# Eight single PSUM banks, 128-row FFN tiles for a second block, and a new written-out order in a fused attention and gated FFN kernel

## The chip, the cores and the metric

The kernel runs on one core of a Trainium2 chip, alone. The metric is the device time of one execution in microseconds, the median of three runs. TensorE is called PE in the profile, VectorE DVE, ScalarE ACT, GpSimd POOL and SyncE SP. PEld is the loading of weights into PE.

## The reference

Block-sparse attention (4 batches, 8 heads, 768 tokens, head width 64), and its output, seen as 3072 tokens of 512 channels, goes through a gated feed-forward network with 1536 inner channels. Cut to what matters:

```python
scores = scale * np.matmul(q, k.transpose(0, 1, 3, 2))          # scale = 1/8
# mask of 32 x 32 blocks: band of 1, first and last row and column, 3 random blocks per row
scores = np.where(mask, scores, -1000000000.0)
attn = softmax(scores)                                           # over keys
out = np.matmul(attn, v)
x = out.transpose(0, 2, 1, 3).reshape(3072, 512)
gate = 1.0 / (1.0 + np.exp(-(x @ w_gate)))
val = x @ w_val
return (gate * val) @ w_out
```

Inputs and output are float32; the mask is the same for all batches and heads.

## The kernel before

All arithmetic on PE is in 16-bit floats with 32-bit sums. The work is cut into 12 units: a unit is one batch and 256 of its 768 queries. In a unit the 8 heads go in 4 pairs (`Pair`), and the keys of a pair in 3 steps of 256 (`Step`).

For one step PE computes scores of 256 keys by 256 queries for both heads (`Step.qk`, 4 matmuls of 64 rows; the two heads lie on the two halves of PE's rows and run together). ACT takes the exponential of the 128x1024 result out of PSUM (`exp`, line 586), DVE multiplies it by the 0/1 mask (`mul`, line 592). In unit 0 the mask isn't ready in time, so there PE adds a bias to the scores instead (matmuls `bias,e`) and DVE does not multiply. When three steps of a pair are done, PE multiplies them by the values, which carry a column of ones (`pv` in unit 0 with 128 rows, `pv_parts` from there on with 64 rows and two partial sums, which DVE adds in `fold`, line 646). DVE divides by the ones column (`norm`, lines 655 and 656), and the result is turned into `xT`: by PE and a copy in units 0 and 1, by a transposing DMA on SP's queue from unit 2 on.

The FFN (`Ffn`) takes units in eight groups, four of one unit (256 tokens) and four of two (512 tokens). `f` computes gate and value sums of 128 inner channels at a time (two times 128 for a group of one unit), ACT takes a tanh (line 801), DVE multiplies (`gate`, line 804) into `ht`. `y` multiplies `ht` by `wo` into 256 output rows, ACT or DVE copies the result to `ysb`, and SP stores it. Group 0 uses PE with all 128 rows (`whole`), the others split the 128 rows into halves that write different PSUM banks (`turns`).

PSUM is held as four tiles `m0` to `m3` of two banks each. Everything that PE writes takes a whole tile, however small it is, and gives it back when it has been read: transposes of 64 columns too.

q, k and v of batch 0 and the weights are loaded by POOL's queue in the fixed order of `FIRST`:

```python
FIRST = "k1 q1 k2 q2 k3 q3 v0 v1 v2 v3 r0 w0 r1 w1 r2 w2 r3 w3 w4 w5 o0 o1 o2"
```

`k1` is k of head pair 1, `q1` the first 256 queries of it, `r0` the other 512 queries of pair 0, `w0` 256 channels of `wg` and then of `wv`, `o0` a third of `wo`. Pair 0's k and first queries come in front of these by SP's and ACT's queues. The loads of later batches are tasks like the others; some wait for a score matmul (a gate, `@` in the order).

The program is written as a list of tasks (`plan.add`), numbered as they are added, each with the engines that may do it and a duration used by a planner outside the program. The order in which tasks are issued is the string `ORDER`: `34:1` is task 34 on PSUM tile 1, `4D` task 4 on DVE, `j3` a matmul on zeros that keeps PE busy. An engine does its tasks strictly in this order: a task that waits holds up all that stand behind it on its engine. The numbers in `plan.add` do not enter the program; only `ORDER` and the task functions do.

Of the kernel before, what the change touches and what calls it, by code (L numbers as in the profile page):

```python
# [16 lines left out]
ALU = mybir.AluOpType  # L17
# [14 lines left out]
PE, ACT, DVE, DMA, SP = "PADGS"  # L32
# [4 lines left out]
EARLY = 2  # L37
# [3 lines left out]
j3 j3 j3 j3 j3 j3 j3 j3 5A 8D j3 0 11A j3s 9:0 j3s j3s j3s 10D j3s j3s 12:1 1:2 j3s 13A 3:0 2 j3s 34:1 4D 35 15:2  # L41
j3s 32:3 16D 6:0 33 17:1 7D 117:2 18D 97:0 118D 44:1 98A j3s 22:3 78:2 23D 45 36:0 79D 20:3 37 21D
40:2 25:1 30:3 41 26D 76:0 77D 46:1 31 54:2 19 74:0 47 75D 27:3 24 55 50:0 28D 80:1 64:3 51 81D
48:2 65 60:1 49 56:0 61 14 66:3 58:2 67D 105@30 57 29 89:3 59 38:1 90 52:0 86:2 53D 87 39 68:3
93:0 69D 62:1 108:2 94 42:3 109 43D 102:0 63D 111:3 70:1 103 110 126:2 71D 112 104 95:0 84:1 96D
122:3 85A 113 140:0 127 123 91 130:1 128 132:3 141 129 131 72:2 119:0 99:1 73D 133 120 147:2 134
100 135 142 157:0 148 154:3 171:1 124 155 149 158 88 164:3 143:2 156 176:0 92@164 144 121 146@111
101 172 170@44 165 173 161:2 217@54 145 190:1 177 189@46 162 125@40 178 237@54 159 186:3 191 150:2
115:0 151D 192 174:2 187 116 204:1 175 188 231:0 179:3 183:2 232 205 180D 244:3 184 233 206 166
245 82:0 200:2 218 83D 201 246 234:3 193:0 219 194A 152 235 185 153 211:2 136:0 220 137D 212 138  # L50
272:3 195 139 229 223A 202 167:0 255:2 168 236 273 213 221A 239 214:0 230 307:1 274 169 215 275
256 240 216 197:3 308 257 196 181 198 258 248:0 309 182 199 241:2 249 242 310 268:3 262 225:1 250
260 114@268 263 269 251 252:2 226 318:0 261 207:3 319 253 315:1 208 289:2 316 160@315 254 106:0
265:3 243 290 107A 247@265 266 270 276:1 209 291 300:0 293:3 277 301 278 282:1 294 292 283 297 163
303:0 335:2 295 302 222 304 279 227 285:1 336 296 286 238 359:0 305 337 360 210 284 331:3 228
362:1 348 332 361 264 349 363 333 328:0 287 350 329 267 322:3 351A 320 344:1 353A 311:0 323
203@344 345 341:2 387:3 321@359 312 342 317 271@282 426:1 373:0 313 411@300 427 330 397:2 374 398
343 388 346 375 259 408:1 376 389 355:2 400@268 409 390 347@30 419:0 356 334@89 380:3 405:1 428
370:2 381 306@111 364 420 288@44 406 371 386@214 366:3 421 410 365@265 454:2 422 433:1 455 432@380
# [3 lines left out]
442 474:1 484:0 463A 378 465A 339 467:2 452 340 475 524:3 480 485 525 514 354 515:1 327 468 486  # L63
# [4 lines left out]
538 583 438 550:1 567 571 542 439 586 551 638:0 563:2 572 425 539 564 552 595:1 573A 404 577:2 604  # L68
639 574 596 578 609:0 568 597 555 575A 627:2 598 616:3 610 628 617 543@616 635:1 565 712@200 630:2
611 569@300 636 612 592:3 446@563 688:0 631 593 658@60 689 654 706:1 556@231 588:3 707 579 641@550  # L70
640 642:0 632 676@471 619:1 633 589 587@282 620 594 691@214 623:2 690 613 590 670:1 591 643 671
637 605:3 624 644 621 606 645 659:1 618 625 709:0 681:3 710 626 660 607 655:2 682 692:0 656 453
663:3 711 726@99 661 657 608@234 673:2 693 662 674 622@652 664 672 694 548 699:1 695 665 723:2 666
# [3 lines left out]
762 669 782 730:3 745A 734:0 760 757:2 731 735 753 798:3 703 758 799 732 736 764:0 759 750 743A  # L77
600 765 797 826:3 823:1 767 763 824 650 816:0 766 651 827 809:1 756 768 810 719 800 787:3 817 769
733 788 806:1 801:0 807 770D 819:3 789 772A 811 737:1 790:2 839 738 614 802 580 615 791 803 601
# [5 lines left out]
904 856 925 936:0 978:1 913 937 911 857 919:3 979 908 875:0 920 914 876 929:1 921 917A 905 932  # L85
970:3 930 935 971 877 922 946:0 915A 1024:3 931 947 893 1025 928 1027:2 1012:0 939 938 916 1013
948 959:3 1028 966 1040:0 940 960 1041 1026 941 967:2 973:3 944A 942D 968 945 1029 952:0 1001:1
# [6 lines left out]
1078 1074 1094 1008 1082 1095 1083 1084 1100:1 1087A 1096A 1108:3 1088 1098A 1101 1085A 1099 1097  # L94
# [3 lines left out]
1163:2 1154D 1164 1159 1156D 1155 1157 1165 1160 1166 1167 1168:0 1161 1169 1170 1162 1171 1172  # L98
"""
GAP, PV_HALF, PV_PARTS, F_HALF, Y_ONE = 0.3, 0.36, 0.74, 0.875, 0.216  # L100
# [14 lines left out]
class Bank:  # L115


    def __init__(self):
        self.slot = None


class Plan:
# [14 lines left out]
    def run(self):  # L137
        done = set()
        for token in self.order:
            if token[0] == "j":  # L140
                self.idle(int(token[1]), token[2:])
                continue
            i, eng, slot, gate = re.fullmatch(r"(\d+)([PADGS]?)(?::(\d))?(?:@(\d+))?", token).groups()
            i = int(i)
            engines, fn, deps, more = self.tasks[i]
            assert i not in done and done.issuperset(deps)
            done.add(i)
            if slot is not None:
                more["take"].slot = int(slot)
# [7 lines left out]
def kernel(  # L157
# [159 lines left out]
    units_ps = [ps.tile([128, 2, 512], f32, name=f"m{i}") for i in range(4)]  # L317

    def both(bank):
        return units_ps[bank.slot]  # L320

    def both16(bank):
        return units_ps[bank.slot].bitcast(f16)

    def idle(unit, kind):
        n = 1 if kind == "s" else 4
        for i in range(2):
            rows = slice(i * D, (i + 1) * D)
            nc.tensor.matmul(
                units_ps[unit][:, i, 0 : n * 128].rearrange("a (x n) -> a x n", n=128),  # L330
# [61 lines left out]
    rings["pr"] = [qp[:, p] for p in range(NP)]  # L392
# [42 lines left out]

    def mask_tiles(c0, c1, j):

        bank = Bank()

        def mm(eng):  # L440
            for i in range(2):
# [716 lines left out]
```

## Time and profile before

| what | value |
|---|---|
| runs | 278.04, 278.94, 278.79 us; median 278.79 us |
| span of the profiled execution, first to last instruction | 277.8 us; the three runs lie 0.2 to 1.1 us above it |
| granted TensorE clock | 0.999 |
| PE busy | 270.0 us (97%), 5007 matmuls |
| DVE busy | 207.1 us (75%) |
| ACT busy | 192.1 us (69%) |
| bytes | 28.47 MB read from HBM, 6.29 MB written |

Busy time is the share of time in which at least one instruction of the engine was under way. Matmuls are pipelined: a matmul is listed with its whole passage, and the distance from one start to the next is what it costs in a stream. "idle before, releaser" in a group says how long the engine had been idle just before such instructions, and what ended it.

### The profile page before, as it was taken

Reading aid. Unit: us, or ns where it says so; the run is one execution under the profiler, and the core shown is the slowest. Engines: PE = TensorE matmul, PEld = TensorE weight load, DVE = VectorE, ACT = ScalarE, POOL = GpSimd, SP = SyncE. Lnnn points to the kernel's source line nnn. Section 1 sums busy time; section 2 is a strip of 40 time slices with the busy share of each in tenths; the row PEclk is TensorE's granted clock in tenths of the full one; section 3 lists DMA queues with packets and bytes.
Section 4 is the critical chain, followed back from the end, with each engine's and each line's share of the span. In section 5 each row is a group of like instructions: output and inputs, shape, how many; then the busy total and the mean of one; then the engine's idle time right before and its main releaser. Section 6 shows DMA issues by size and latency. Waiting matters only on the chain.

```text
span 277.8 us, 11169 instructions
## 1 busy us (share of the span) xinstructions
PE 270.0 (97%) x5007; PEld 178.7 (64%) x5007; DVE 207.1 (75%) x421; ACT 192.1 (69%) x243; POOL 47.3 (17%) x69
## 2 busy tenths in 40 slices
PE   8879999999999999999999999999999999999995
PEld 3667785896897798655566655655655676555543
DVE  4667788899999989978988886887876899004422
ACT  3988868899989958968868965679688571035300
POOL 7776261030480000028300000000000000000000
PEclk9999999999999999999999999999999999999999
DMA  7999999994599693339986743014130002230004
GB/s 160 175 195 197 200 205 198 140 139 100 84 160 145 117 140 97 103 98 167 142 113 113 73 61 97 2 21 142 24 96 4 4 2 76 70 151 2 0 2 151
DMA packets 56684, 28.93 MB, mean 104 GB/s; under 512 B 33036, under 2 KB 53692, under 8 KB 56636
## 3 DMA queue, kind: packets, MB, share of 16 engines
q0 software_dynamic: 21520, 13.90, 35.7%
q1 hardware_dynamic: 34628, 14.02, 24.8%
q8 instruction: 39, 0.64, 1.0%
q10 hardware_dynamic: 488, 0.30, 0.3%
q14 instruction: 9, 0.07, 0.1%
HBM read 28.47 MB, written 6.29 MB: 125 GB/s over the span
## 4 chain that ended last, share of the span: by engine, by line
PE 87%; DMA 7%; POOL 2%; ACT 1%; DVE 1%; issue 1%; SPq 0%
PE m L352 86%; DMA q<-in_q_dram 3%; DMA v<-in_v_dram 2%; DMA kT<-kp 1%; ACT P L586 1%; POOL k L226 1%; POOL q L226 1%; POOL wg L236 0%; POOL wv L236 0%; DVE ysb L888 0%; DVE P L592 0%; ACT ysb L886 0%; PE m L472 0%; PE m L467 0%; ACT ysb L929 0%
## 5 line engine op out<-in xcount | busy, mean ns | idle before, releaser
L586 ACT ACTIVATE P<-m 128x1024 f16<-128x1024 f32 x144 | 143.1, 1025 | 27.8 <-PE m L352 24.6
L352 PE MATMUL m<-xT,wg 64*128 64x512 f16 (+2 forms) x720 | 136.7, 326 | 0.1
L352 PE MATMUL m<-xT,wv 64*128 64x512 f16 (+2 forms) x720 | 136.7, 326 | 0.0
L592 DVE TENSOR_TENSOR P<-P,mask 128x1024 f16<-128x1024 f16 x132 | 87.0, 684 | 2.7 <-ACT P L586 2.6
L352 PEld LDWEIGHTS <-wg 64*128 64x128 f16 (+1 forms) x720 | 66.6, 94 | 21.2 <-issue 0.8
L352 PEld LDWEIGHTS <-wv 64*128 64x128 f16 (+1 forms) x720 | 66.4, 94 | 18.2 <-issue 0.5
L804 DVE SCALAR_TENSOR_TENSOR ht<-th,m 128x512 f16<-128x512 f32 x72 | 49.0, 685 | 37.0 <-ACT th L801 36.1
L352 PE MATMUL m<-wo,ht 64*128 64x512 f16 (+2 forms) x564 | 70.4, 372 | 0.0
L801 ACT ACTIVATE th<-m 128x512 f32<-128x512 f32 x72 | 42.8, 598 | 29.6 <-PE m L352 26.1
L352 PE MATMUL m<-qT,kT 64*128 64x256 f16 x576 | 53.6, 269 | 0.9 <-DMA kT<-kp 0.5
L352 PEld LDWEIGHTS <-P 64*128 64x128 f16 (+1 forms) x2112 | 41.1, 94 | 5.2 <-issue 0.4
L352 PEld LDWEIGHTS <-ht 64*128 64x128 f16 (+1 forms) x564 | 29.4, 94 | 23.4 <-issue 1.3
L352 PE MATMUL m<-vex,P 64*128 64x65 f16 (+1 forms) x2112 | 42.5, 190 | 0.0
L352 PEld LDWEIGHTS <-kT 64*128 64x128 f16 x576 | 26.7, 94 | 17.8 <-issue 1.3
L646 DVE TENSOR_REDUCE acc<-m 128x260 f32<-128x520 f32 x40 | 27.8, 697 | 7.9 <-PE m L352 6.8
L226 POOL DMA_DIRECT2D k<-in_k_dram x15 | 11.1, 744 | 48.3 <-PE m L352 45.0
L886 ACT ACTIVATE ysb<-m 128x512 f32<-128x512 f32 x18 | 10.2, 601 | 11.8 <-PE m L352 11.8
L656 DVE TENSOR_TENSOR x<-acc,rz 128x256 f16<-128x256 f32 x40 | 17.0, 425 | 1.4
L226 POOL DMA_DIRECT2D v<-in_v_dram x16 | 11.6, 736 | 33.5 <-PE m L352 12.9
L226 POOL DMA_DIRECT2D q<-in_q_dram x19 | 13.9, 733 | 3.9 <-DMA wo<-in_moe_w_out_dram 1.8
L352 PE MATMUL m<-bias,e 64*128 64x256 f16 x48 | 5.9, 271 | 2.3 <-DVE mask L299 1.9
L929 ACT ACTIVATE ysb<-m 128x256 f32<-128x256 f32 x1 | 0.4, 383 | 10.1 <-PE m L352 10.1
(47 smaller groups left out, 84.1 us busy)
## 6 DMA issues: line engine op xcount, KB each, us to landing
out_dram<-ysb SPq DMA_DIRECT2D x23, 256.0 KB, 2.4
v<-in_v_dram POOLq DMA_DIRECT2D x16, 192.0 KB, 5.1
k<-in_k_dram POOLq DMA_DIRECT2D x15, 192.0 KB, 6.6
q<-in_q_dram POOLq DMA_DIRECT2D x12, 192.0 KB, 6.4
wg<-in_moe_w_gate_dram POOLq DMA_DIRECT2D x6, 256.0 KB, 8.4
wv<-in_moe_w_val_dram POOLq DMA_DIRECT2D x6, 256.0 KB, 9.0
wo<-in_moe_w_out_dram POOLq DMA_DIRECT2D x3, 512.0 KB, 12.8
xT<-x SPq DMA_TRANSPOSE x40, 2.4
```

Of the source, the lines that this page charges most:

```text
L226: return nc.gpsimd.dma_start(dst[:, h0:h1, t0:t1, :], src[b, h0:h1].rearrange("h (p t) d -> p h t d", t=NT)[:, :, t0:t1, :],)
L352: return nc.tensor.matmul(out, lhsT, rhs, start=start, stop=stop, skip_group_check=True).ins
L586: nc.scalar.activation(self.pt.rearrange("a h i n -> a (h i n)"), both(self.bank).rearrange("a h n -> a (h n)"), AF.Exp, bias=0.0, scale=SCALE
L592: nc.vector.tensor_tensor(self.pt, self.pt, m.unsqueeze(1).broadcast_to([128, 2, 2, UQ]), op=ALU.mult,)
L646: nc.vector.tensor_reduce(self.acc.rearrange("a h s d -> a (h s d)"), self.parts.rearrange("a r n -> a n r"), axis=mybir.AxisListType.X, o ...
L656: nc.vector.tensor_tensor(self.x16.rearrange("a s h d -> a h s d"), self.acc[:, :, :, 0:D], rz.broadcast_to([128, 2, 2, D]), op=ALU.mult,)
L801: nc.scalar.activation(th, both(bank)[:, 0, :], AF.Tanh, bias=0.0, scale=0.5)
L804: nc.vector.scalar_tensor_tensor(self.ht[:, tiles[0] : tiles[-1] + 1, :], in0=th.rearrange("a (f n) -> a f n", n=self.w), scalar=1.0, in1= ...
L886: nc.scalar.activation(ysb, both(bank)[:, s, :], AF.Copy, bias=0.0, scale=0.5)
L929: nc.scalar.activation(ysb, src, AF.Copy, bias=0.0, scale=0.5)
```

## The change

Four things change in the program; line numbers here are of the kernel before.

1. PSUM is one tile of eight banks. A task takes either a pair of banks (slots 0 to 3, as before) or a single bank (slots a to h). The small products move to single banks: transposes of q, k and x in the first units, the value product of unit 0, mask and bias rows in part, and the last output rows.
2. Transposes in a single bank use PE with 128 rows: one matmul for a 128x128 piece instead of two or four of 64 rows, and the copy out of PSUM becomes contiguous. Transposes that keep a pair of banks stay as they were.
3. Groups 0 and 1 of the FFN (`SMALL = 2`) use a new task `f1`: 128 inner channels for 256 tokens, gate and value beside each other in one bank, with 128 rows. Each has a tanh and a gate product of 256 columns, so 12 instructions of 512 columns become 24 of 256 on ACT and on DVE. In the kernel before, group 1 used halves of rows and group 0 128 rows with two banks. Four of them (`EARLY = 4`) begin before the last quarter of `xT`.
4. `ORDER` is new. Its first 620 tasks are ordered with other durations and with loads and PE's instruction transfers taken into account; about half of the tasks stand in another sequence and partly on other engines, and the last 2412 of PE's matmuls in the same sequence as before; there are 1205 tasks instead of 1173. `FIRST` is the same, and so are all loads. The loads of batch 1 are gated one by one instead of in a block.

The numbers in `plan.add` change as well, without effect on the program. The diff, cut to the core:

```diff
-EARLY = 2
+EARLY, SMALL = 4, 2
 ORDER = """
-j3 j3 j3 j3 j3 j3 j3 j3 5A 8D j3 0 11A j3s 9:0 j3s j3s j3s 10D j3s j3s 12:1 1:2 j3s 13A 3:0 2 j3s 34:1 4D 35 15:2
...
+8 j2 j2 j2 j2 j2 j2 j2 j2 j2s j2s 9:0 5A 10A 6Q:c 0 j2s 1:d 11 12:2 13A 3:3 4A 2 7 j0s 32:0 33
+30:1 15Q:g 31 16 17Q:h 18 34:2 74Q:a 82Q:b 83 44:3 35 45 75 40:1 41 20Q:b 21 27Q:e 22Q:f 23 28
...
-    units_ps = [ps.tile([128, 2, 512], f32, name=f"m{i}") for i in range(4)]
+    banks = ps.tile([128, 8, 512], f32, name="m")
+    units_ps = [banks[:, 2 * i : 2 * i + 2, :] for i in range(4)]
...
+    def one(bank):
+        i = "abcdefgh".index(bank.slot)
+        return units_ps[i // 2][:, i % 2, :]
...
-    def halves(out16, tiles):
+    def turned_in(bank, tiles):
...
+            if bank.single:
+                if flat:
+                    nc.tensor.transpose(one16(bank)[:, i * 128 : (i + 1) * 128], tile_, ident)
...
     def pv(self, eng):
-            acc = both(self.bank)[:, :, 0 : 2 * (D + 1)]
...
+            self.acc = one(self.bank)[:, 0 : 4 * (D + 1)].rearrange(
+                "a (h s d) -> a h s d", h=2, s=2
+            )
...
+        def f1(self, f):
+            bank = Bank()
...
+                    for c in cs:
+                        for g in range(2):
+                            bank.last = tiled(
+                                one(bank)[:, g * UQ : (g + 1) * UQ],
+                                (wg, wv)[g][:, c, f * 128 : (f + 1) * 128],
+                                self.x[:, c, :],
+                                c == 0 and g == 0,
+                                c == 3 and g == 1,
+                            )
+            def tanh(eng):
+                nc.scalar.activation(th, one(bank)[:, 0:UQ], AF.Tanh, bias=0.0, scale=0.5)
+            def gate(eng):
+                nc.vector.scalar_tensor_tensor(
+                    self.ht[:, f, :], in0=th, scalar=1.0, in1=one(bank)[:, UQ : 2 * UQ],
+                    op0=ALU.add, op1=ALU.mult,
+                )
...
         def f(self, j):
+            if self.g < SMALL:
+                for f in range(self.per * j, self.per * (j + 1)):
+                    self.f1(f)
+                return
```

More of the change, by code (lines that the diff above doesn't have):

```diff
@@ L31 @@
 NU = S // UQ
-PE, ACT, DVE, DMA, SP = "PADGS"
+PE, ACT, DVE, DMA, SP, ONE = "PADGSQ"
 VB = 5
@@ L46 @@
[L46 to L51, printed above, removed]
@@ L438, in mask_tiles, with half @@
         bank = Bank()
+        w = c1 - c0
+        def half(i):
+            return one(bank)[:, i * w : (i + 1) * w] if bank.single else both(bank)[:, i, 0:w]
         def mm(eng):
@@ L548, in go @@
             )
-        a = plan.add([(DVE, 0.4)], go, deps + read.get(("pv", b - 2, p), []))
+        a = plan.add([(DVE, 0.268)], go, deps + read.get(("pv", b - 2, p), []), needs=(f"v{p}",) if b == 0 else ())
         copies.setdefault(("v", b, p), []).append(a)
@@ L748, in scores @@
             take=run[0][1].bank,
-            ops=16 if first else 8,
+            score=True,
+            needs=("e0", "e1") if first else (),
         )
@@ L753, in scores @@
             e = plan.add(
[L754 removed]
+                [(ACT, 0.903)], st.exp, [a] + before("P", 3 * pr.i + st.j), free=st.bank
             )
@@ L844, in f @@
                     take=bank,
-                    lag=GAP,
-                    ops=16 * self.per,
+                    needs=wneeds,
                 )
                 a = plan.add(
-                    [(PE, F_HALF)], half(False), [a], ops=16 * self.per
+                    [(PE, 0.863 if self.w == 512 else 0.872)], half(False), [a], turn=True
                 )
             used["xT"][self.g].append(a)
-            c = plan.add([(ACT, 0.57)], tanh, [a] + before("th", i), free=bank, part=1)
-            g = plan.add([(DVE, 0.68)], gate, [c], free=bank, part=1)
+            old = before("th", i)
+            if i < len(rings["th"]) and used["th1"]:
+                old = [x for m in (2 * i, 2 * i + 1) for x in used["th1"][max(k for k in used["th1"] if k % 6 == m)]]
+            c = plan.add([(ACT, 0.477)], tanh, [a] + old, free=bank)
+            g = plan.add([(DVE, 0.598)], gate, [c], free=bank)
             used["th"][i] = [g]
@@ L898, in part @@
                     take=bank if first and f0 == 0 else None,
-                    lag=0.0 if f0 < 8 else GAP if first else None,
-                    ops=16,
+                    turn=not first and f0 == 0,
+                    needs=(f"o{f0 // 4}",),
                 )
```

306 lines of the change are left out of this document (172 added, 134 removed), and 51 rows, old and new, of the table ORDER.

## The prediction

> **What bounds the kernel now.** I read the table of windows first, to see in which stretch PE is short of work.
>
> ```profile
> span 277.8 us, 11169 instructions
> core 0: us, PE busy (x) PEld busy (x) DVE busy (x) ACT busy (x) POOL busy (x), PEclk, DMA share, GB/s
> 0.00:24.00 24.00, 19.99 (x438) 13.71 (x439) 14.70 (x41) 17.80 (x21) 17.75 (x28) 1.00 1.21 180
> 24.00:43.00 19.00, 18.94 (x283) 14.88 (x280) 15.25 (x32) 14.34 (x19) 8.76 (x14) 1.00 1.35 201
> 43.00:103.00 60.00, 60.00 (x1428) 47.87 (x1426) 54.88 (x112) 53.43 (x67) 11.42 (x16) 1.00 0.93 134
> 103.00:151.00 48.00, 47.48 (x960) 30.51 (x956) 41.65 (x84) 38.21 (x48) 9.33 (x13) 1.00 0.71 122
> 151.00:275.00 124.00, 123.56 (x1918) 71.73 (x1912) 80.65 (x155) 68.20 (x92) 0.00 (x0) 1.00 0.21 53
> ```
>
> From 24 us on PE is idle for 0.06 + 0 + 0.52 + 0.44 = 1.0 us in all: the body is bound by PE at full clock. So only two things can move the end: how much of PE's work is done by the time that it is saturated, and stalls that a new order puts into the body. What a matmul costs in a stream, and where the start-up ends, the timeline of PE tells:
>
> ```profile
> 23.69 0.32 PE L472 MATMUL m<-const,q 64*64 64x64 f16 x16 [0.23 <-DMA q<-in_q_dram]
> 23.94 0.28 PE L352 MATMUL m<-xT,wg 128*128 128x256 f16 x1
> 24.06 0.27 PE L352 MATMUL m<-xT,wv 128*128 128x256 f16 x1
> 24.17 0.27 PE L352 MATMUL m<-xT,wg 128*128 128x256 f16 x1
> 25.16 0.27 PE L352 MATMUL m<-xT,wv 128*128 128x256 f16 x1
> 25.36 0.23 PE L467 MATMUL m<-const,x 64*128 64x64 f16 x4
> 26.75 0.89 PE L352 MATMUL m<-vex,P 128*128 128x65 f16 x24
> 27.48 0.28 PE L352 MATMUL m<-xT,wg 128*128 128x256 f16 x1
> 42.57 1.03 PE L352 MATMUL m<-wo,ht 64*128 64x512 f16 x8
> 43.43 0.38 PE L352 MATMUL m<-qT,kT 64*128 64x256 f16 x4
> 43.65 0.59 PE L352 MATMUL m<-wo,ht 64*128 64x512 f16 x4
> ```
>
> From start to start: 0.11 us for an FFN matmul of 256 columns, 0.73/24 = 0.030 for a whole-row value matmul, 0.22/4 = 0.055 for a score or bias matmul, 0.86/8 = 0.108 for one with `wo`, 0.25/16 = 0.016 for a small transpose. In program order there stand before the first FFN matmul (23.94) 116 score and bias matmuls, 96 value matmuls, 14 of the mask and 172 transposes: 6.4 + 2.9 + 1.5 + 2.8 = 13.6 us of work. The rest of those 24 us is lost, and this is what a new order can give back. Where it is lost:
>
> ```profile
> 6.73 1.94 ACT L586 ACTIVATE P<-m 128x1024 f16<-128x1024 f32 x2 [0.86 <-PE m L352]
> 8.56 0.59 ACT L297 CAST mask<-m 128x512 f16<-128x512 f32 x1
> 9.17 5.69 ACT L586 ACTIVATE P<-m 128x1024 f16<-128x1024 f32 x6
> 16.01 4.82 ACT L586 ACTIVATE P<-m 128x1024 f16<-128x1024 f32 x5 [1.15 <-PE m L352]
> 12.13 0.69 DVE L299 CAST mask<-m 128x512 f16<-128x512 f32 x1
> 14.35 0.36 DVE L545 COPY vex<-v 128x768 f16<-128x768 f16 x1 [1.53 <-DMA v<-in_v_dram]
> 14.63 0.68 DVE L299 CAST mask<-m 128x512 f16<-128x512 f32 x1
> 15.36 0.29 PE L352 MATMUL m<-bias,e 64*128 64x256 f16 x2 [1.91 <-DVE mask L299]
> ```
>
> DVE stood before a copy of v that had not landed, with a mask copy behind it; PE waited 1.91 us for the PSUM tile under that mask, and ACT then 1.15 us for scores. Exponentials come 0.93 us apart when fed ((5.69 - 1.03)/5).
>
> **The change part by part.**
>
> *To the first FFN matmul.* Loads stay as they are. In the new order DVE does four mask copies before it waits for the first v, and the next score has a free bank meanwhile, so the 1.91 and the 1.15 go. ACT does one mask copy less here (0.49), but takes the first k copy and the 768-column mask row in front of its first exponential; PE's first bias waits for DVE anyway, so I leave the first exponential at 6.7 (up to 0.5 later). Twelve at 0.93 with 0.3 of small waits: the last ends at 18.2, where it ended at 16.01 + 4 x 0.95 = 19.8. Behind it come 0.73 of values, 0.6 of DVE's norm, transposes and a copy of 0.3; the transposes of the second half of q1 stand in between. The first FFN matmul starts at about 20.8 instead of 23.94. What is late next: the q2 transposes, which PE now reaches before their load. That load ended a wait at 23.69 above, so PE stands there until then, behind two FFN tiles.
>
> *To the last third of `wo`.* The loads run at a fixed pace: POOL's next issue waits for the load eight places before it.
>
> ```profile
> 40.42 0.72 POOL L226 DMA_DIRECT2D k<-in_k_dram  x1 [1.77 <-DMA wo<-in_moe_w_out_dram]
> 42.95 0.71 POOL L226 DMA_DIRECT2D q<-in_q_dram  x1 [1.81 <-DMA wo<-in_moe_w_out_dram]
> ```
>
> So the last third of `wo` lands shortly before 42.95, and PE first uses it at 43.65, the third row of `wo` above being its start. Up to that use the old order has, since the first FFN matmul, 96 FFN, 48 score, 96 value, 16 `wo`, 2 mask matmuls and some transposes, 18.6 us, in 19.7. The new one has 96, 76, 96, 16 and some transposes, and 48 split value matmuls at half price (0.7): 20.8, with 1.1 of small losses as before 21.9, from 20.8 to 42.7. Both the work and the load give 42.7 to 42.9; I take 42.9, 0.75 earlier than 43.65. And PE has then done more: 24 more scores (1.3) and the 48 value matmuls (0.7), less two mask matmuls (0.2): 1.8. Together 2.55 us ahead. ACT allows it: up to there PE needs 33 exponentials (30.7 at 0.93), 12 halved tanh (3.6 at the 0.3 that an estimate from 383 ns and overlap gives) and nothing else after 6.7, so 41.0 without a pause, 1.9 of room. Bounds: 2.8 if PE stands ready when the load lands, about 0.5 if ACT pauses and feeds PE 2 us later. Loads of batch 1 are issued earlier, but behind `wo` on the same queue.
>
> *The body.* The order is new for the first two fifths of PE's work; the last 2412 matmuls, from about 123 us on, stand in the same sequence as before and cost what they cost. Work for PE is the same but for 128-row shapes. Here a rule speaks against the change: row 25.16 to 25.36 is 0.20 where a step is 0.11, 0.09 for leaving the 128-row shape. [...] The new order enters or leaves the 128x128 shape 31 times instead of 23, +0.7; between the third `wo` use and the common sequence it changes from one kind of job to another 15 times less, and such a change costs between nothing (row 43.43 to 43.65 is 0.22 for four scores, as elsewhere) and that same 0.09: 0 to -1.4. I take -0.3 (0.7 to -0.8).
>
> DVE and ACT get more:
>
> ```profile
> L804 DVE SCALAR_TENSOR_TENSOR ht<-th,m 128x512 f16<-128x512 f32 x72 | 49.0, 685 | 37.0 <-ACT th L801 36.1
> L801 ACT ACTIVATE th<-m 128x512 f32<-128x512 f32 x72 | 42.8, 598 | 29.6 <-PE m L352 26.1 <-DVE acc L646 2.7 <-DVE ht L804 0.8
> L931 DVE TENSOR_SCALAR ysb<-m 128x512 f32<-128x512 f32 x1 | 0.7, 692 | 0.4 <-PE m L352 0.4
> L931 DVE TENSOR_SCALAR ysb<-m 128x256 f32<-128x256 f32 x1 | 0.4, 425 | 1.0 <-PE m L352 1.0
> L929 ACT ACTIVATE ysb<-m 128x256 f32<-128x256 f32 x1 | 0.4, 383 | 10.1 <-PE m L352 10.1
> ```
>
> Half the columns cost 425 of 692 ns on DVE and 383 of 598 on ACT, so twelve instructions cut in two cost 12 x 0.158 = 1.9 us on DVE and 12 x 0.168 = 2.0 on ACT. [...] Three output copies go from ACT to DVE before 100 us (3 x 0.69 = 2.1). So DVE has some 4 us more by then, and in the windows 24 to 103 it idles 3.75 + 5.12 = 8.9 us. That idle covers the 4 us; for the part that falls at a wrong moment I charge a twelfth, 0.35. For waits that a new order may bring in elsewhere, of which the old one had 1.0 after 24 us, I add 0.3; ends 0 and 5.
>
> Sum: -2.55 - 0.3 + 0.65 = -2.2; since the first term is taken near the good end of its bounds, I go by -1.9. The span of 277.8 becomes 275.9. The profiled run's time isn't given apart; the three runs lie 0.2 to 1.1 above this span, and I move their median: 278.8 - 1.9 = 276.9.
>
> **The rivals.** (a) *All of it arrives.* PE stands at the load of `wo`, no stall is new: -2.8 - 0.8, 275.2. For it: PE's idle of 1.0 us in the 251 from 24 on shows that a written order can do it. (b) *ACT keeps the start-up.* If ACT pauses some 2 us between 21 and 43 us (in the window 24 to 43 it now idles 19.00 - 14.34 = 4.66), using up its room and the lead of the first 21, PE comes to `wo` at 44.9, 1.25 late with 1.8 ahead: -0.5, 278.3, no change. (c) *DVE becomes the bound.* In 43 to 103 it is busy 54.88 of 60 us already, and the idle that is left may all be waits for exponentials and tanh. Then its 4 us come on top, with 1 us for stalls that follow at PE's banks: +5 - 2.55 = +2.4, 281.2. It decides from the point at which more than 2.55 of the 4 us find no idle time. Against it: the same 60 us have PE without any gap. (d) *The order does nothing,* since PE is saturated: excluded from 24 us on only; the 24 us before have 10 to give.
>
> **How the numbers follow.** Forecast 276.9 with chance 0.46 (275.8 to 278.0), (a) 0.19, (b) 0.16, (c) 0.19. A measurement here can tell 0.3% from no change, 0.84 us: faster is below 277.95. Faster: 0.43 + 0.19 + 0.02 = 0.64; same: 0.03 + 0.13 = 0.16; slower: 0.01 + 0.19 = 0.20. The range takes (a) to 275.2 and half of (c), to 280.3; about 0.15 is outside.
>
> **What would show it.** Right: no PE wait over 1 us on `mask` before 16 us; the first 128-row FFN matmul at 20.5 to 21.3; the third `wo` group at 42.7 to 43.5; PE idle under 1.7 us after 24 us. (b) would show ACT waiting for PE between 20 and 40 us. (c) would show PE released by DVE's `acc`, `ht` or `P` again and again between 43 and 103 us, and DVE at 57 of 60 us. Wrong: an FFN start at 23 us or later, or a span over 277.

## The result, and the profile after

| | median of runs | ratio to the kernel before |
|---|---|---|
| kernel before | 278.59 us (278.04 to 278.94, 6 runs) | |
| changed kernel | 281.08 us (279.74 to 283.02, 6 runs) | 1.010, 95% interval 1.0065 to 1.0136 |

The changed kernel is slower by 0.7 to 1.4%, where 276.9 us had been forecast. Its profiled execution took 282.22 us and spans 280.5. In every run that lists both, of either kernel, the time is 1.7 to 1.85 us above the span. The forecast did not have this, and it matters below.

The table of windows of the changed kernel, with the same columns as before:

```profile
core 0: us, PE busy (x) PEld busy (x) DVE busy (x) ACT busy (x) POOL busy (x), PEclk, DMA share, GB/s
0.00:24.00 24.00, 22.46 (x392) 16.58 (x393) 16.22 (x45) 20.09 (x24) 18.51 (x29) 1.00 1.21 178
24.00:43.00 19.00, 19.00 (x328) 14.85 (x326) 17.17 (x40) 17.73 (x27) 7.95 (x11) 1.00 1.35 202
43.00:103.00 60.00, 55.61 (x1164) 45.86 (x1162) 52.43 (x116) 46.36 (x64) 11.49 (x16) 1.00 1.04 145
103.00:151.00 48.00, 47.90 (x980) 34.78 (x977) 41.54 (x79) 35.36 (x45) 9.29 (x13) 1.00 0.68 99
151.00:275.00 124.00, 124.00 (x1974) 77.78 (x1970) 81.43 (x158) 70.75 (x94) 0.00 (x0) 1.00 0.20 52
```

One row is out of line: from 43 to 103 us PE, which had no gap there before, is idle for 4.39 us. DVE is busy for less of it than before (52.43 against 54.88), and it had kept up then, so it is not the bound. What PE waited for after 24 us:

```profile
PE m L366 <- issue: 2.6, 2, 2.5
PE m L366 <- DMA kT<-kp: 1.7, 1, 1.7
```

And where, in the timeline of PE (in brackets the idle time before the row and what ended it):

```profile
21.00 0.27 PE L366 MATMUL m<-xT,wg 128*128 128x256 f16 x1
43.11 1.04 PE L366 MATMUL m<-wo,ht 64*128 64x512 f16 x8
57.80 0.61 PE L366 MATMUL m<-qT,kT 64*128 64x256 f16 x8 [1.74 <-DMA kT<-kp]
79.78 0.28 PE L366 MATMUL m<-xT,wg 64*128 64x256 f16 x1 [0.20 <-issue]
87.62 0.28 PE L366 MATMUL m<-xT,wv 64*128 64x256 f16 x1 [2.45 <-issue]
```

The first FFN matmul (21.00) and the first use of the third of `wo` (43.11) come where the forecast had them. Then PE loses 1.9 us, from start to start, to the transposing DMA of k for the first scores of the second batch, and 0.46 and 2.72 us in the middle of two runs of FFN matmuls where it waits for no semaphore ("issue").

What these two have in common is the DMA queues. DMA issues between 70 and 90 us (KB of each, median us from issue to landing), of the kernel before and then of the changed one:

```profile
q<-in_q_dram POOLq DMA_DIRECT2D x4, 192.0 KB, 6.4
xT<-x SPq DMA_TRANSPOSE x4, 3.6
```

```profile
q<-in_q_dram POOLq DMA_DIRECT2D x4, 192.0 KB, 8.5
out_dram<-ysb SPq DMA_DIRECT2D x3, 256.0 KB, 7.2
xT<-x SPq DMA_TRANSPOSE x4, 8.4
```

The kernel before issues no transposing DMA from 69.6 to 83.3 us, while most of its loads run; the changed kernel issues two transposes (74.5 and 75.8 us) and two stores in the middle of ten loads, and each of these two transposes takes 8.4 us. The 3.6 of the kernel before is the middle of two landings, 4.4 and 2.9 us; the trace has none for the other two. The transposes into kT between 44 and 64 us show the same (before, then after):

```profile
DMA to landing us min/median/max: 3.3/3.6/3.9
```

```profile
DMA to landing us min/median/max: 2.5/5.2/7.8
```

These are one profile each. In the two later profiles of the kernel before (they come at the end of the experiments) the landings are 4.2 to 5.0 us, in the later one of the changed kernel up to 6.3.

The stalls on "issue" come from PE's own instructions. The page lists them as a queue:

```profile
q8 instruction: 38, 0.62, 0.9%
```

38 packets of 16 KB for 9692 matmuls, weight loads and the few others of PE: 255 to a packet. I numbered PE's instructions in the trace. The stalls stand at 2752 and 3008, which are 256 apart and both 192 beyond a multiple of 256, and the packets that PE must have waited for ended 1.4 us before it went on. In quiet stretches a packet starts when PE is some 180 beyond a multiple of 256; these two started 4.7 and 6.4 us later than that. Of the wait for such a packet up to 2.72 us lay open.

### The profile page after: what moved, and what is told of

It reads as the page before. It is cut to its first block, busy times and chain, and to the rows that moved or that the text cites. A ratio compares the mean times of both kernels' runs of the same rounds, so it can differ in the third digit from the quotient of the medians.

```text
span 280.5 us, 10847 instructions
## 1 busy us (share of the span) xinstructions
PE 271.3 (97%) x4837; PEld 191.3 (68%) x4837; DVE 209.9 (75%) x436; ACT 190.7 (68%) x252; POOL 47.2 (17%) x69
## 4 chain that ended last, share of the span: by engine, by line
PE 91%; DMA 4%; issue 1%; DVE 1%; ACT 1%; DVEq 0%
PE m L366 90%; DMA kT<-kp 3%; DMA e<-bb_spread 1%; PE m L489 1%; ACT P L622 0%; DVE ysb L976 0%; DVE P L628 0%; PE m L499 0%; PE m L502 0%; ACT th L902 0%; DVE kp L561 0%; DVE bias L439 0%; ACT ysb L1016 0%; DVE e L212 0%; DVE qT L304 0%
## 5 line engine op out<-in xcount | busy, mean ns | idle before, releaser
L622 ACT ACTIVATE P<-m 128x1024 f16<-128x1024 f32 x144 | 141.4, 1030 | 24.9 <-PE m L366 24.3
L366 PEld LDWEIGHTS <-wg 64*128 64x128 f16 (+1 forms) x672 | 62.3, 95 | 19.3 <-issue 1.5
L366 PEld LDWEIGHTS <-wv 64*128 64x128 f16 (+1 forms) x672 | 62.4, 95 | 17.7 <-issue 2.7
L905 DVE SCALAR_TENSOR_TENSOR ht<-th,m 128x512 f16<-128x512 f32 x60 | 40.9, 686 | 32.5 <-ACT th L902 31.7
L902 ACT ACTIVATE th<-m 128x512 f32<-128x512 f32 x60 | 35.7, 598 | 29.5 <-PE m L366 25.5
L366 PEld LDWEIGHTS <-ht 64*128 64x128 f16 (+1 forms) x564 | 32.8, 94 | 21.3 <-issue 1.3
L366 PEld LDWEIGHTS <-kT 64*128 64x128 f16 x576 | 30.5, 94 | 15.8 <-issue 2.1
L974 ACT ACTIVATE ysb<-m 128x512 f32<-128x512 f32 x14 | 7.9, 598 | 12.2 <-PE m L366 12.2
L831 ACT ACTIVATE th<-m 128x256 f32<-128x256 f32 x24 | 8.8, 402 | 6.3 <-PE m L366 5.3
L834 DVE SCALAR_TENSOR_TENSOR ht<-th,m 128x256 f16<-128x256 f32 x24 | 9.2, 416 | 2.3 <-ACT th L831 2.3
```

The lines of the kernel that those rows point to most:

```text
L366: return nc.tensor.matmul(out, lhsT, rhs, start=start, stop=stop, skip_group_check=True).ins
L622: nc.scalar.activation(self.pt.rearrange("a h i n -> a (h i n)"), both(self.bank).rearrange("a h n -> a (h n)"), AF.Exp, bias=0.0, scale=SCALE
L831: nc.scalar.activation(th, one(bank)[:, 0:UQ], AF.Tanh, bias=0.0, scale=0.5)
L834: nc.vector.scalar_tensor_tensor(self.ht[:, f, :], in0=th, scalar=1.0, in1=one(bank)[:, UQ : 2 * UQ], op0=ALU.add, op1=ALU.mult,)
L902: nc.scalar.activation(th, both(bank)[:, 0, :], AF.Tanh, bias=0.0, scale=0.5)
L905: nc.vector.scalar_tensor_tensor(self.ht[:, tiles[0] : tiles[-1] + 1, :], in0=th.rearrange("a (f n) -> a f n", n=self.w), scalar=1.0, in1= ...
```

## The experiments

The theory: (S1) transposing DMAs of q and k take twice as long where loads run beside them, and PE waits for kT; (S2) loads together with SP's transposes and stores delay PE's instruction packets, and PE runs dry. All edits are in `ORDER` (a task number with `@` waits for the score task named there), and `Pair.xbar` returns its instruction so that it can be held.

Each edited kernel was profiled once, and what is said of waits and packets is of that one execution; the times are medians.

**Place of one load, place of two transposes, number of instructions.** Four kernels. The first, k0_second, loads k of pair 0 earlier:

```diff
 105@56
+92@56
...
-92@165
```

> The changed kernel with one load moved: k of head pair 0 of the second batch is issued second of its batch (right behind q of pair 0) instead of sixth. Theory (place in the queue): its transpose into kT starts some 4 us earlier, TensorE's wait of 1.91 us at 55.87 us for that transpose is gone, the rest is as before: 279.2 us against 281.1. Rival (transposes slowed by the loads still under way until 54 us, wherever k stands): the transpose still takes 7 to 8 us to land, the wait stays over 1 us, and the time is 280.5 to 281.1.

Measured: 280.06 us, ratio 1.0064 (1.0031 to 1.0098). Waits of PE:

```profile
PE m L366 <- DMA kT<-kp: 2.1, 1, 2.1
PE m L366 <- issue: 1.6, 1, 1.6
```

The wait on kT stayed (the transpose took 7.8 us again). It doesn't decide on the place of the load: DVE's copy and SP's transpose kept their places in the order, at 50 us, so the earlier load could hardly help. The profile is also of one of the two longest of the ten runs (283.01 us): in it the granted clock stood at 0.5 from 58.6 to 62.0 us, right behind the wait for kT, with a mean of 0.993, where the eight runs of 279.4 to 280.3 us have 0.998 to 1.000.

xt_late holds two transposes back:

```diff
-423 ... 370
 475:3
+370@475 423@475
```

> The changed kernel with the two transposing DMAs of attention results that SyncE issued at 74.5 and 75.8 us, amid the ten loads of the third batch, held back until the score matmuls at 83.9 us. Theory (transposing DMAs among loads slow the DMA engines, and TensorE's next 16 KB of instructions come late): the loads move at 160 KB/us or more from 72 us on, no instruction transfer starts over 3.5 us after TensorE has reached instruction 180 of its 256, the two stalls of 0.41 and 2.67 us within a run of FFN matmuls at 79.3 and 84.9 us are gone: 278.0 us against 281.1. Rival (ten loads in a row are enough, the transposes do nothing): both stalls stay, 280.5 to 281.5.

(`423` and `370` are the transposes; SP keeps their order in what follows.) Measured: 279.41 us (278.42 to 280.11, 10 runs), ratio 1.0022 (1.0000 to 1.0044). No stall on "issue" after 24 us is left; the latest packet in 60 to 100 us is 3.3 us late. The rate of the loads did not come as expected (111 to 135 KB/us between 72 and 80 us), and a wait of 0.9 us for kT remains.

shift96 puts 96 instructions in front:

```diff
-j2
+j2s j2s j2s j2s
```

(eight times, at the start)

> The changed kernel with eight of the idle matmul pairs at the start cut into four pieces each: the same columns, 96 TensorE instructions more ahead of everything else. Theory (TensorE runs out of fetched instructions): stalls without a semaphore come at TensorE's instructions number 2752 and 3008 again (192 beyond a multiple of 256), 96 instructions earlier in the program than in the changed kernel, or at other numbers 256 apart from these. Rival (something at that place of the program, a bank or a mode): they come at the same matmuls, now number 2848 and 3104. Time 279 to 282 us by both.

Measured: 281.24 us, ratio 1.0078 (1.0042 to 1.0114). The stalls, in the timeline of PE:

```profile
77.57 0.28 PE L367 MATMUL m<-xT,wg 64*128 64x256 f16 x1 [1.40 <-issue]
84.86 0.28 PE L367 MATMUL m<-xT,wg 64*128 64x256 f16 x1 [1.92 <-issue]
```

They are at PE's instructions 2752 and 3008, the same numbers, which are now other matmuls of the program, 96 earlier. This settles that PE waited for instructions.

k0_xt has the edits of k0_second and xt_late:

> Both edits together: k of head pair 0 loaded second, and the two transposing DMAs held back until 83.9 us. Theory: both losses go, 1.9 us and 3.1 us, and the gain of some 2 us that the start has made by 52 us stays to the end: 276.1 us against 281.1, below the kernel before (278.6). Rivals of either part: 278 where one of the two losses stays, 281 where both stay.

Measured: 279.51 us, ratio 1.0022 (0.9999 to 1.0045). Waits of 0.8 us for kT and 1.1 us on "issue" are left: neither edit did its part in full.

**Loads moved instead.** v_later holds three loads of v back:

```diff
-267@108 ... 114@261 ... 171@254
 289:0
+114@289 267@289
 333:0
+171@333
-174 ... 288
 249
+174 288
```

(`174` and `288` are DVE's copies of v of pairs 0 and 3.)

> The changed kernel with three loads of v of the second batch (v of head pairs 3, 0 and 1, issued at 34.7, 43.3 and 46.1 us) held back to score matmuls at 57.9 and 59.7 us, and the copies of two of them put behind. Theory (the transposing DMAs of q and k are slow because loads run to 54 us beside them): loads end by 51.5 us, the transpose into kT issued at 49.95 us lands in 5 us or less instead of 7.8, TensorE's wait of 1.91 us at 55.9 us falls under 0.5: 279.4 us against 281.1 (the stalls at 79 and 85 us stay). Rival (it is issued too late, 49.95 us against 48.13 in the kernel before, and takes its time anyway): the wait stays over 1 us, 280.5 to 281.1.

Measured: 279.43 us, ratio 1.0021 (0.9992 to 1.0051). The wait for kT is gone, the transposes land in 4.1 to 5.0 us. Another wait of PE takes its place, since DVE stands before a v copy whose load is late. PE from 55 to 75 us, then DVE from 57 to 66:

```profile
PE m L366 <- DVE acc L682: 1.3, 1, 1.3
```

```profile
DVE vex L581 <- DMA v<-in_v_dram: 0.8, 1, 0.8
```

loads_76 holds the third batch's loads back and leaves SP alone:

```diff
-295@330 ... 353@394 ... 464@394 ... 366@426 ... 314@426 ... 418@360
 347:2
+295@347 353@347 464@347 366@347 314@347 418@347
-409
+409@429
-306
 328
+306
```

(`306` is DVE's copy of k of pair 0, `328` that of q.)

> The changed kernel with the ten loads of the third batch that it issued from 68.8 to 79.9 us all held back to the score matmuls at 76.4 us, and the one transposing DMA of attention results that would fall among them (83.9 us) held to 88.6 us: no transposing DMA is issued between 76 and 88 us. Theory (loads beside SyncE's transposing DMAs and stores delay TensorE's instruction transfers): none of these starts over 3.7 us after TensorE reached instruction 180 of its 256, the stalls at 79 and 85 us (0.41 and 2.67 us) are gone: 278.0 us against 281.1. Rival (ten loads in a row are enough by themselves): a stall of over 0.5 us at TensorE's instruction 2752, 3008 or 3264, and 279.5 us or more.

Measured: 284.94 us, ratio 1.0209 (1.0157 to 1.0260). No stall on "issue"; but DVE waited for a q load, and PE for DVE:

```profile
DVE qp L561 <- DMA q<-in_q_dram: 4.0, 1, 4.0
```

Not all of the 6.4 us over the kernel before is this wait. PE stood 3.6 us for DVE and 1.3 for kT, and behind the 3.6 the granted clock was 0.5 from 88.0 to 91.4 us; the mean is 0.994 in the profiled run and 0.988 in the other three. The same is seen in v_l76 and v_quiet, 3.4 us at 0.5 behind waits of 3.9 and 2.3 us, and in before_78, 6.9 us at 0.5 in and behind a wait of 5.6; it is not seen in the first profile of the changed kernel behind 2.45 us, nor in v_quiet2 behind 2.8. Half the clock for 3.4 us is, as an estimate from these two numbers, a loss of some 1.7 us. In all six runs of the changed kernel the mean clock is 0.999 or more, so this is no part of what is explained here.

v_l76 is v_later and loads_76:

> The last two edits together. Theory: both losses are gone, 1.9 and 3.1 us, and the lead of about 2 us over the kernel before that there is at 52 us stays to the end: 276.2 us against 281.1, and against 278.5 of the kernel before. Rivals: 278 where one of the losses stays, 281 where both do.

Measured: 284.38 us, ratio 1.0194 (1.0146 to 1.0243), with the same wait of DVE.

before_78 is the kernel before with

```diff
-321@359 271@282 411@300 400@268 347@30 334@89
 380:3
+321@380 271@380 411@380 400@380 347@380 334@380
```

> The kernel before with eleven of its loads, of the third batch but for three of v of the second, held back from 72.3 us to the score matmuls at 78.0 us, so that they run to 90 us, over the three transposing DMAs at 83.3 to 86.6 us. Theory (loads and transposing DMAs together make TensorE's instructions late, in any order of tasks): an instruction transfer starts over 4 us after TensorE reached instruction 180 of its 256 where the longest in the body was 2.7 us, and a stall without a semaphore of 0.5 to 3 us appears at an instruction 192 beyond a multiple of 256, near 88 or 95 us: 279 to 281.5 us against 278.5. Rival (the stall belongs to the new order of tasks): no such stall, 278.2 to 278.8.

Measured: 285.64 us, ratio 1.0239 (1.0191 to 1.0288). It doesn't decide: the packet there was 3.9 us late, as the theory has it, but PE had no stall on "issue", since it stood 5.6 us for DVE, which waited 6.9 us for a q load. It did show one thing that I hadn't asked for: up to 77 us it is the same program as the kernel before, and it was 0.96 us ahead of that kernel's profile from 24 us on.

**Both, with less side effect.** v_two loads v of pair 0 in the place of pair 3:

```diff
-267@108 ... 114@261 ... 171@254
+114@108
 289:0
+267@289
 333:0
+171@333
-288
 259
+288
```

> The changed kernel with v of head pair 0 loaded in the place of v of pair 3 (34.7 us) in the second batch, and v of pairs 3 and 1 held to the score matmuls at 57.9 and 59.7 us: two loads fewer beside the transposing DMAs of q and k. The kernel with three held back lost its wait on kT at 55.9 us and got one of 1.6 us at 62 us, where VectorE waited for the load of a v copy; here the copies have their loads in time. Theory: the wait on kT (1.91 us) is under 0.5 and none of over 0.5 us takes its place before 70 us: 279.2 us against 281.1, with the stalls at 79 and 85 us left. Rival (seven q and k loads are enough to slow the transposes): the wait stays over 1 us, 280.3 or more.

Measured: 279.98 us, ratio 1.0051 (1.0023 to 1.0079). No wait for kT is left and none over 0.6 us before 70 us; 1.6 us of stall at instruction 3008 remain. The transposes into kT between 44 and 64 us:

```profile
DMA to landing us min/median/max: 3.7/4.1/4.6
```

S1 holds: two loads fewer beside them, and the transposes are in time. All profiles of the changed order agree: between 46 and 65 us the longest landing of a transpose into kT is 4.3 to 5.0 us in the seven kernels that hold loads of v back (v_two, v_later and those made from them) and 6.3 to 7.8 us in the nine profiles without. How much of that is the transpose's own is not told apart: in the first profile of the changed kernel two transposes of q stand in front of it on SP's queue and take 8.6 and 7.3 us.

sp_quiet holds all of SP's queue:

```diff
-357 ... 384 ... 242 ... 423 ... 370
 475:3
+357@475 384 242 423 370
```

> The changed kernel with the whole of SyncE's queue held from 69 us to the score matmuls at 83.9 us (three transposing DMAs of attention results and two stores of outputs), and the ten loads left where they are. Theory (loads beside SyncE's DMAs): the loads have the DMA engines to themselves, no instruction transfer between 70 and 90 us starts over 3.5 us after TensorE reached instruction 180 of its 256 (4.7, 6.4 and 5.2 in the changed kernel), no stall without a semaphore: 278.0 us against 281.1, and with less spread. Rival (ten loads are enough): stalls of over 0.5 us at instructions 2752 or 3008 stay, 279.5 or more.

Measured: 281.45 us, ratio 1.0097 (1.0073 to 1.0120). The stalls are gone, and PE, from 70 to 110 us, waits for a transpose that came late behind the held ones:

```profile
PE m L366 <- DMA qT<-qp: 1.3, 1, 1.3
```

v_quiet is v_two and sp_quiet:

> The last two edits together. Theory: both losses are gone, the lead of some 2 us at 52 us stays to the end: 276.2 us against 281.1, below the kernel before (278.5), a ratio of 0.990 to 0.994. Rivals: 278 where one of the losses stays, 280 or more where both do.

Measured: 282.46 us, ratio 1.0133 (1.0110 to 1.0157): 2.3 us for qT near 105 us, and a stall of 0.5 us at 3008 although SP moved nothing while that packet waited.

loads_76b is loads_76 with DVE's copies `306 328 371` put behind `424`, and `410` behind `346`.

> The kernel with ten loads held to 76.4 us once more, with the four copies on VectorE that depend on the late ones put behind the loads' landing (in the first form VectorE waited 4.0 us for a load, and TensorE 3.8 us for VectorE, while the stalls without a semaphore were gone). Theory: the stalls stay away (instruction transfers at most 3 us behind) and nothing replaces them: 278.0 us against 281.1. Rival (later loads come too late for the third batch whatever the order): VectorE or SyncE waits for loads again, or the scores at 105 us wait for kT, 280 or more.

Measured: 280.71 us, ratio 1.0078 (1.0057 to 1.0099). The stalls at 79 and 85 us are gone. The loads now run to 94 us and meet SP's transposes there, and the stall is there too, at instruction 3520, again 192 beyond a multiple of 256:

```profile
96.65 0.60 PE L366 MATMUL m<-wo,ht 64*128 64x512 f16 x3 [1.14 <-issue]
```

That is what before_78 had been meant to show: in these profiles the stall follows the meeting of loads and SP's DMAs, and not the tasks.

**Is that all?** v_xt is v_two (with the copy `288` a little later) and xt_late; v_xt3 holds `357` as well; v_quiet2 is v_quiet with `307@475 329` in front of the held ones.

> The edit of v_two (two v loads fewer beside the transposing DMAs of q and k; one copy of v a little later than there) and that of xt_late (two transposing DMAs held to 83.9 us) together. If the two losses are all: no wait on kT over 0.5 us at 56 us, stalls without a semaphore under 0.5 us together, 277.0 us against 281.1 and 278.6 of the kernel before. If the loads keep instruction transfers late in part, as where k of pair 0 was moved together with the two transposes (1.5 us left): 278.3. If something else is lost: 279 or more with neither in the trace.

> As v_xt, with a third transposing DMA, the one issued at 69.5 us as the loads begin, held to 83.9 us too; SyncE's two stores stay at 73 us. If transposing DMAs are what delays loads and instruction transfers: stalls without a semaphore under 0.3 us, 276.8 us. If the stores delay them as well: 0.5 to 1.5 us of stalls, 278. A rival: the transposes behind come late and the scores at 101 to 105 us wait 1 to 3 us for qT, as where the whole queue was held: 279 or more.

> As v_quiet (all of SyncE's queue held from 69 to 83.9 us), with the transposes of q and k of head pair 0 of the third batch put in front of what was held, since the scores at 105 us waited 2.4 us for them. If that wait was all that v_quiet had in place of the two losses: 277.2 us against its 282.5. Rival: the other transposes are as late now, and TensorE waits for them at 101 to 110 us instead: 280 to 282.

Measured: v_xt 278.77 us (ratio 0.9992, 0.9965 to 1.0019), v_xt3 279.45 us (1.0016, 0.9991 to 1.0040), v_quiet2 282.66 us (1.0150, 1.0103 to 1.0197). In v_quiet2 there is no stall on "issue", but 2.8 us for qT near 106 us (four of its six runs have a mean granted clock of 0.994, the profiled one 1.0). In v_xt3, with no transpose left among the loads but two stores, 0.8 us of stall remain, so transposes alone are not the cause. v_xt has, after 24 us, only this:

```profile
PE m L366 <- issue: 0.5, 1, 0.5
```

That makes v_xt the best version of the new order, and no better than the kernel before. So something else separates 276.9 from 278.8. The start was left, and each kernel was profiled again (before_b, before_c, after_b):

> The kernel before, unchanged, profiled once more. If the first profile had a slow start (the first v load late): TensorE's wait for the mask near 14 us is 0 to 0.7 us instead of 1.91, the first FFN matmul starts at 23.0 to 23.4 instead of 23.94, the span is 276.5 to 277.2 and the time 278.2 to 278.9. If that start is the rule: wait 1.7 to 2.1 us, FFN at 23.8 to 24.1, span 277.6 or more.

> The kernel before, unchanged, a third profile; the same as for the second.

> The changed kernel, unchanged, profiled once more. If its losses are as the first profile has them: the first 128-row FFN matmul at 20.3 to 21, a wait of 0.7 to 2.3 us for kT near 56 us, stalls without a semaphore of 1.5 to 4 us together at TensorE's instructions 2752, 3008 or others 192 beyond a multiple of 256, and by these sums a time between 279.7 and 283.

Measured, one run each: 278.14, 277.71 and 280.00 us (spans 276.4, 275.9, 278.2). The two new profiles of the kernel before, PE's timeline, before_b and then before_c:

```profile
14.53 0.29 PE L352 MATMUL m<-bias,e 64*128 64x256 f16 x2 [0.60 <-DVE mask L299]
22.90 0.28 PE L352 MATMUL m<-xT,wg 128*128 128x256 f16 x1
```

```profile
14.23 0.28 PE L352 MATMUL m<-bias,e 64*128 64x256 f16 x2 [0.74 <-DVE mask L299]
22.81 0.28 PE L352 MATMUL m<-xT,wg 128*128 128x256 f16 x1
```

The wait of 1.91 us is 0.6 to 0.7 in them, and the first FFN matmul comes a little earlier than expected. The v load that DVE copies first (the second of the four to be issued) landed at 14.33 us in the profile of the prediction, at 12.49 in before_b and at 13.19 in before_c. DVE stood 1.53 us before that copy in the first, 0.35 in before_c and not at all in before_b:

```profile
13.21 0.35 DVE L545 COPY vex<-v 128x768 f16<-128x768 f16 x1
```

And the changed kernel once more (after_b), PE after 24 us. The stall is in the expected range; the wait for kT is not (0.7 to 2.3 us had been expected), so it differs much between executions of one program:

```profile
PE m L366 <- issue: 1.8, 1, 1.8
PE m L366 <- DMA kT<-kp: 0.2, 1, 0.2
```

Put together, worked out from the traces: the time at which PE has done so much work of its own (matmul columns at the steps of the prediction; the changed order has 0.85 us more of them, all in the start, left out here), against the first profile of the kernel before. A minus is ahead of it.

```
work done, us        12     40     50     65     75    105    250
before, first     24.17  54.32  64.80  80.35  90.66 121.83 271.69
before_b          -1.05  -1.06  -1.06  -1.06  -0.72  -0.79  -1.48
before_c          -1.13  -1.13  -1.14  -1.14  -1.14  -1.21  -1.91
after, first      -3.85  -2.09  +0.05  +0.43  +3.39  +3.25  +2.61
after_b           -3.55  -1.79  -1.18  -1.18  +1.09  +0.96  +0.34
v_xt              -3.86  -1.45  -1.21  -1.20  -0.16  -0.30  -0.94
```

Against the other two profiles of the kernel before, the changed one is 0.7 to 1.0 us ahead at 40 us of work, not 2.1. It then loses 0.6 to 2.1 us up to 50 (the wait for kT) and 2.3 to 3.0 from 65 to 75 (instruction packets). v_xt, with hardly any of these, ends 0.5 to 1.0 us behind them.

And for S2: the latest instruction packet between 60 and 100 us in each profile, with what the loads under way still had to move when it was due, what SP's queue moved while it waited (both roughly), and the stalls on instructions from 60 to 100 us (start to start, over 0.3 us).

```
              late, us   loads, KB   SP, KB   stalls, us
before          2.3         669         0     -
before_b        4.2         683         0     0.35
before_c        2.7         632         0     -
loads_76        2.8          71       449     -
v_quiet2        3.0         596         0     -
v_quiet         4.3         601         0     0.53
xt_late         3.3         724        96     -
sp_quiet        3.3         763       108     -
v_xt            4.2         658        53     0.80
v_xt3           4.5         623       206     1.07
k0_xt           5.0         558       128     0.83 + 0.80
v_two           4.9         546       142     1.58
v_later         5.4         552       176     1.11 + 1.08
k0_second       5.2         573       209     1.90
loads_76b       4.4         175       661     1.51
after, first    6.4         639       362     0.46 + 2.72
after_b         5.4         624       414     2.10
shift96         7.2         304       643     1.66 + 2.18
```

In this table loads with none of SP's DMAs or up to 110 KB of them make a packet 2.3 to 4.3 us late, loads with 120 KB and more 4.4 to 7.2; the stalls begin at some 4 us. The border is not sharp: counted from the very instruction 180, SP's share is 78 KB in k0_xt and 104 in v_two; another packet of v_xt3 was 4.5 us late with some 30 KB of SP's, and one of before_78 3.9 us with some 160. SP's DMAs with a single load beside them do little: 2.8 us in loads_76, and 1.7 for a packet of v_quiet2 with 477 KB. What holds without a border are the stalls by what was held back from the ten loads: all of SP's queue, 0 to 0.53 us (sp_quiet, v_quiet, v_quiet2); two or three transposes, 0 to 1.63 (xt_late, v_xt, v_xt3, k0_xt); nothing, 1.58 to 3.84 (v_two, k0_second, v_later, shift96 and both profiles of the changed kernel). So the rival "ten loads are enough" was right in a small part (v_quiet, before_b), and most of the stall belongs to the meeting. How the meeting makes a packet late is not shown: no run here shows which DMA engine carried the packet and what stood before it, and stores and transposes were not told apart.

## Why the prediction was wrong, step by step

**To the first FFN matmul: right for the changed kernel, wrong for the other side.** 20.8 us was forecast (20.5 to 21.3 as the sign); it came at 21.00, and at 21.31 in the second profile. No wait on a mask over 1 us is left. But the 23.94 that this was set against was one execution in which the v load that DVE copies first came late. In the others the kernel before is at 22.8 to 22.9. The step that failed is "the 1.91 and the 1.15 go": a wait that ends on a DMA was taken from one profile as a fixed property, 1.1 us too large. The wait for the load of q2, which was forecast next, is in neither profile of the changed kernel: from 18 to 45 us PE has no wait of over 0.1 us at all.

**To the last third of `wo`: the same.** Forecast 42.9, measured 43.11 (43.42 in the second profile), with 24 scores and 48 split value matmuls more and two mask matmuls fewer done, 1.8 us by the prediction's own steps: 2.3 ahead of the first profile, forecast 2.55. The kernel before is there at 42.5 and 42.6 in its other profiles, so the lead over those is 0.9 to 1.3, and 0.7 to 1.0 at 40 us of work in the table. ACT was no hindrance, rival (b) is out: between 20 and 43 us it waited 0.9 us for PE in all, after 5.3 in the kernel before.

**The median.** "The profiled run's time isn't given apart; the three runs lie 0.2 to 1.1 above this span, and I move their median": with 1.7 us above the span as in every run here, that execution took some 279.5 us, 0.7 above the median. Its excess of 1.1 us at the start was counted as a gain to be had, and then taken off a median that holds at most part of it.

**The body, modes and jobs.** Forecast -0.3 (0.7 to -0.8); its two parts, +0.7 and 0 to -1.4, have their middle at 0, so the -0.3 has no working. Other rows of the first profile of the kernel before agree with the 0.09 us behind the +0.7: leaving the 128-row shape, 0.20 to 0.21 us from the last start to the next (28.68 and 31.77 us), where a step is 0.11; entering it, 0.54 us from the first of eight scores to the next FFN matmul (29.14 and 31.97 us), where eight are 0.44. From 40 us of work to the end, after_b loses 2.9 us on before_c, which has no stall on instructions; 2.5 of it are the wait for kT (0.4) and the stall (2.1). For the first profile of the changed kernel it is 5.5, and 5.1. So +0.4 remains in both against before_c, of the other sign, within the bounds; against before_b, which has a stall of 0.35 us itself, it is next to nothing.

**DVE, 0.35.** The cover held: DVE is not among the waits after 24 us, and rival (c), DVE as the bound, is wrong as a mechanism; that its 281.2 us lie beside the measured 281.08 is chance.

**"Waits that a new order may bring in elsewhere", 0.3 with ends 0 and 5.** This is the step that turned the sign: 5.1 us in the first profile, 2.5 in the second (2.1 of stalls and 0.4 for kT). The 0.3 was set by the 1.0 us of idle time in the old order, and not worked out from the new one. It left out two things that the order moves on the queues: SP's transposes against POOL's loads, and the packets of PE's instructions. It had the issue times of both queues in the old trace, and the new order of both.

The sum with the measured terms, for after_b against before_c: lead -0.7, kT +0.4, stalls +2.1, body +0.4, together +2.2, where it ends 2.25 behind. The medians are 2.5 apart. The sum is of one profile of each side. Rival (a) fell with the stalls.

## What to carry to other kernels

A gain that is read off an idle time in one profile should first be looked for in a second profile of the same kernel, above all where the wait ends on a DMA; and the time of that profile has to be known before anything is taken off a median. When an order is rewritten, set POOL's loads and SP's transposes and stores against each other in time, and count PE's instructions: a stall on "issue" in the middle of a run of equal matmuls is tested by numbering the instructions, and by adding some in front. Moving a load on one queue moves whatever stands in order behind its consumer: seven of the kernels here cured one wait and got another (in loads_76 no stall on "issue" was left, and PE stood 3.6 us for DVE).

## What the runs showed of the hardware that was not expected

- PE's program comes in packets of 16 KB (38 for 9692 matmuls, weight loads and the few others in the changed kernel, 255 to a packet). Between 60 and 100 us they started up to 7.2 us after PE had passed instruction 180 of its 256 (shift96), latest where loads and SP's DMAs met. PE had some 4 us of cover there: no stall at 3.3 us of delay, 0.35 us at 4.2. All stalls without a semaphore of over 0.4 us between matmuls after 24 us stood 192 beyond a multiple of 256 (2752, 3008, 3520).
- A transposing DMA of q or k (128 x 768 16-bit values, 192 KB) issued between 46 and 65 us landed in 2.5 to 4.6 us where no load moved a byte meanwhile (kT at 64.0 us in the changed kernel, qT at 50.8 us in the kernel before), and in up to 7.8 us (kT, first profile of the changed kernel) and 8.8 us (qT, shift96) where several loads did; holding two loads of v back was enough for 3.7 to 4.6 (kT in v_two).
- The same load of one and the same program landed at 12.49, 13.19 and 14.33 us in three executions of the kernel before; in the last, everything that follows is 1.1 us later up to 65 us of work.
- Behind waits of PE of 2.1 to 5.6 us the granted clock stood at 0.5 for 3.4 to 6.9 us in five profiles (k0_second, loads_76, v_l76, v_quiet, before_78), and at 1.0 behind 2.45 and 2.8 us in two others (the first of the changed kernel, v_quiet2). What decides is not shown.
